# Third PSUM bank for the first mixing in the last chunk, and x of the first batch and its first MLP products ahead of that chunk

## The chip, the cores and the metric

The kernel runs on one core of a Trainium2 chip. The metric is the device time of one execution in microseconds (us), as a median over runs. Five engines work side by side, each in the order in which its instructions are written: PE (TensorE, matrix products), DVE (VectorE), ACT (ScalarE), POOL (GpSimd), and SP, which here only issues DMA transfers. They wait for each other through semaphores. PSUM, into which PE writes its products, has eight banks of 2 KiB per partition.

## The reference

Talking-heads attention over 4 batches, 12 heads, 448 positions and head size 64, and then an MLP over its 1792 tokens (768 to 2048 to 768), all in float32:

```
scores = scale * np.matmul(q, k.transpose(0, 1, 3, 2))
scores = np.einsum('bhij,hg->bgij', scores, w_pre)
scores = scores - np.max(scores, axis=-1, keepdims=True)
attn = np.exp(scores)
attn = attn / (np.sum(attn, axis=-1, keepdims=True) + 1e-09)
attn = np.einsum('bhij,hg->bgij', attn, w_post)
x = np.matmul(attn, v)        # then heads are joined: (B * S, H * D)
...
h = x @ w_in
r = np.maximum(h, 0.0)
out = (s * (r * r) + b) @ w_out
```

## The kernel before

**Tiling.** A batch's 448 rows are cut into four chunks of 110, 110, 110 and 118 rows, 16 chunks (0 to 15) in all; a chunk is cut into blocks of up to 10 rows x 12 heads, which fill 120 partitions. There are 180 blocks, 0 to 179; the last chunk, 15, has blocks 168 to 179 (the last two have 108 partitions). Step `s` of one long loop (L775 to L808) begins the first mixing of block `s` and carries the earlier blocks on.

**A block's way.** `relayout` (five steps ahead) has SP load a block of scores (`blk`); `split` (two steps ahead) has POOL cut it into a high and a low half (`hl`, L555 and L556). `premix(s)` is the first mixing: three PE products into a PSUM bank `pm` (L568), DVE's maximum over a row (L570), ACT's exponential with its sum (L575) and a small ACT operation on the sum (L579). In the next step `normalize(s-1)` takes the reciprocal on DVE (L587) and has ACT write the high half of the result, `eh` (L589); `remainder(s-1)` has DVE write its low half (L596), which is the last reading of the bank. `postmix(s-2)`, the second mixing, is 12 small products with `eh` (L611), and `evacuate(s-3)` copies them to `A`, on DVE (L627), for the last chunk on ACT (L625). AV products, `xp` (L509), turn a chunk's `A` and `v` into x^T, which ACT scales to `xs` (L523) and SP writes to memory (`xd`, L528).

**Banks.** The first mixing takes turns among three banks (two `pm`, one `px`) in all chunks but the last, where it has the two `pm` alone (L565).

**The MLP's beginning.** Three of the MLP's first products, called the head (`ph_head`, for the first batch and f = 0, 1, 2; each has six pieces, kc = 0 to 5, of three PE products), are put into the attention's last steps. The two scores banks are free by then and hold f = 0 and 1; `px` holds f = 2, whose pieces come after the last block. They need x of the first batch: `load_x` reads it back (`xraw`, L210), `split_x` has ACT write its high half (L224) and puts the low half (a DVE subtraction, L233) on a list that `low_parts` empties in the next step, between `normalize` and `evacuate`. x of the second batch takes the same `xraw` buffers, so its load waits for that subtraction. After step 168 DVE also converts MLP weights, three operations in a step (L155 to L178), until 10 units are done.

**What sets the order.** Each engine's order is that of the code. AV pairs and head pieces are spread over the steps by a planner (`fill`): a piece has a wanted step, a first and a last step and a cost, and a step takes pieces until 1.33 are spent. `tail` is 168.

Of the kernel before, what the change touches and what calls it, by code (L numbers as in the profile page):

```python
# [21 lines left out]
def talking_heads_attention__then__act_relu2_kernel(  # L22
# [27 lines left out]
    NKC = DM // P  # L50
# [11 lines left out]
    NCH = len(chunks)  # L62
# [3 lines left out]
    first = []  # L66
# [9 lines left out]
    NB = len(blocks)  # L76
# [106 lines left out]
    def convert_step(upto):  # L183

        if done["run"] is None:
            if done["conv"] >= min(upto, len(units)):
                return False
            done["run"] = conversion(done["conv"])
        try:
            next(done["run"])  # L190
        except StopIteration:
            done["run"] = None
            done["conv"] += 1
        return True
# [13 lines left out]
    def load_x(r, b, kc):  # L208
        raw = rp.tile([P, S], F32, tag="xraw", name=f"xraw_{r}_{b}_{kc}", bufs=NKC)
        nc.sync.dma_start(raw, xd[b][kc])  # L210
        xraw_t[r, b, kc] = raw

    def split_x(r, b, kc):
        raw = xraw_t.pop((r, b, kc))
        if b == 1:

            if kc % 2 == 0:
                x_u["g"] = mp.tile(
                    [P, 2, PT], F32R, tag=f"g{kc // 2}_1", name=f"xg_{r}_{kc}", bufs=1
                )  # L220
            x = x_u["g"][:, :, kc % 2 * S:kc % 2 * S + S]
        else:
            x = rp.tile([P, 2, S], F32R, tag="x", name=f"x_{r}_{b}_{kc}", bufs=NKC)
        nc.scalar.activation(x[:, 0, :], raw, AF.Copy)  # L224
        later.append((x[:, 1, :], raw, x[:, 0, :]))
        x_u[r, b, kc] = x
# [3 lines left out]
    def low_parts():  # L230
        while later:
            o, x, hi = later.pop(0)
            nc.vector.tensor_tensor(out=o, in0=x, in1=hi.bitcast(F32), op=ALU.subtract)  # L233
# [35 lines left out]


    NHEAD = 3
    head_t, head_todo = {}, [(f, kc) for f in range(NHEAD) for kc in range(NKC)]

    def head_piece():
        if not head_todo:
# [267 lines left out]
    def relayout(t):  # L543
        ci, i0, ni = blocks[t]
        blk = blkp.tile([BP, S], F32, tag="blk", name=f"blk_{t}", bufs=LD)
        nb = first[ci + 1] - first[ci]
        r = t - first[ci]
        nc.sync.dma_start(blk[:ni * H, :], s_t[ci][r:r + nb * (ni - 1) + 1:nb, :, :])
        blk_t[t] = blk

    def split(t):
        n = blocks[t][2] * H
        blk = blk_t.pop(t)
        hl = blkp.tile([BP, 2, S], F32R, tag="hl", name=f"hl_{t}", bufs=2)
        nc.gpsimd.tensor_scalar(hl[:n, 0, :], blk[:n], 1.0, 0.0, op0=ALU.mult, op1=ALU.add)  # L555
        nc.gpsimd.tensor_tensor(  # L556
            out=hl[:n, 1, :], in0=blk[:n], in1=hl[:n, 0, :].bitcast(F32), op=ALU.subtract
        )
        hl_t[t] = hl

    def premix(t):
        n = blocks[t][2] * H
        hl = hl_t.pop(t)

        tag = "px" if t % 3 == 2 and t < first[NCH - 1] else "pm"  # L565
        pm = ps.tile([P, 512], F32, tag=tag, name=f"pm_{t}", bufs=banks.count(tag))
        for m, (w, x) in enumerate(((wpre_lo, 0), (wpre_hi, 1), (wpre_hi, 0))):
            nc.tensor.matmul(pm[:n, :S], w[:n, :n], hl[:n, x, :], start=(m == 0), stop=(m == 2))  # L568
        st = smp.tile([BP, 4], F32, tag="st", name=f"st_{t}")
        nc.vector.tensor_reduce(  # L570
            out=st[:n, 0:1], in_=pm[:n, :S], axis=AX.X, op=ALU.max, negate=True
        )

        e = pm[:, :S]
        nc.scalar.activation(e[:n], e[:n], AF.Exp, bias=st[:n, 0:1], accum_out=pm[:n, S:S + 1])  # L575
        e_t[t] = (e, st)

        total = pm[:, S:S + 1]
        nc.scalar.activation(  # L579
            st[:n, 2:3], total[:n], AF.Identity, scale=2.0 ** -15, bias=tiny[:n]  # L580
        )

    def normalize(t):

        n = blocks[t][2] * H
        e, st = e_t[t]
        nc.vector.reciprocal(st[:n, 3:4], st[:n, 2:3])  # L587
        eh = blkp.tile([BP, 2, S], F16, tag="eh", name=f"eh_{t}", bufs=2)
        nc.scalar.activation(eh[:n, 0, :], e[:n], AF.Copy, scale=st[:n, 3:4])  # L589
        eh_t[t] = eh  # L590

    def remainder(t):
        n = blocks[t][2] * H
        e, st = e_t.pop(t)
        eh = eh_t[t]
        nc.vector.scalar_tensor_tensor(  # L596
            out=eh[:n, 1, :], in0=e[:n], scalar=st[:n, 3:4], in1=eh[:n, 0, :],
            op0=ALU.mult, op1=ALU.subtract,
        )

    def postmix(t):
        ci, i0, ni = blocks[t]
        n = ni * H
        eh = eh_t.pop(t)
        if i0 == 0:
            a_t[ci] = ap_.tile([P, NC, H, CH], F32, tag="A", name=f"A_{ci}")
        po = ps.tile([P, 512], F32, tag="po", name=f"po_{t}", bufs=2)
        for c in range(NC):
            j0 = min(c * P, S - P)
            for m, (x, y) in enumerate(((1, 0), (0, 1), (0, 0))):  # L610
                nc.tensor.matmul(  # L611
                    po[:, c * BP:(c + 1) * BP],
                    eh[:n, x, j0:j0 + P],
                    wpost[:n, y].rearrange("p g i -> p (g i)"),
                    start=(m == 0),
                    stop=(m == 2),
                )
        po_t[t] = po

    def evacuate(t):  # L620
        ci, i0, ni = blocks[t]
        dst = a_t[ci][:, :, :, i0:i0 + ni]
        src = po_t.pop(t)[:, :NC * BP].rearrange("p (c g i) -> p c g i", c=NC, g=H)[:, :, :, :ni]
        if ci == NCH - 1:
            nc.scalar.activation(dst, src, AF.Copy)  # L625
        else:
            nc.vector.tensor_copy(dst, src)  # L627

    LD, LS = 5, 2
# [9 lines left out]
    def at(step, order, f, *args):  # L639
        plan.append((step, order, len(plan), f, args))  # L640
# [16 lines left out]
    fill = []  # L657
    for ci in range(2, NCH):
        b, _, _ = chunks[ci]
        w0 = first[ci - 1] - LD  # L660
# [4 lines left out]
        for p in range(NP):  # L665
            when = w0 + p * (w1 - w0) / NP
# [6 lines left out]
    for ci in range(NCH):  # L673
        b = chunks[ci][0]
        w0 = first[ci + 1] + 3
        w1 = first[ci + 2] + 3 if ci + 2 <= NCH else NB + 100
        if ci == NCH - 1:
            w0 = NB + 3
        for p in range(NP):
            when = w0 + p * min(w1 - w0, 12) / NP  # L680
            fill.append((when, w0, w1 - 1, AV_COST, 1, av_pair, (ci, p)))
            if b + 1 < B and chunks[ci + 1][0] != b:
                at(w0 + (p + 1) * (w1 - w0) / NP, 2, load_v, b + 1, p)
    w0 = first[NCH - 1] + 3
    for i in range(NHEAD * NKC):
        if i < NHEAD * NKC - LATE:
            when = w0 + i * (NB + 3 - w0) / (NHEAD * NKC - LATE)
            fill.append((when, w0, NB + 2, 0.567, 1, head_piece, ()))
        else:
            fill.append((NB + 100, NB + 3, NB + 100, 0.567, 1, head_piece, ()))  # L690
    fill.sort(key=lambda x: x[0])
    spent, closed = 0.0, {}
    for s in range(NB + 4):
        spent = max(spent, -0.4) + load.get(s, 0)
        left, held = [], set()
        for x in fill:
            _, lo, hi, cost, order, f, args = x
# [16 lines left out]
        fill = left  # L714
# [5 lines left out]
    def run_plan(step, early):  # L720

        k0 = state["next"]
        while k0 < len(plan) and plan[k0][0] < step + 1:
            _, order, _, f, args = plan[k0]
            if (order == 0) == early:
                f(*args)
            k0 += 1
        if not early:
            state["next"] = k0
# [44 lines left out]
    tail = first[NCH - 1]  # L774
    for s in range(NB + 3):  # L775
        if s == tail - LD:
            early.close()
            rp = ctx.enter_context(tc.tile_pool(name="rp", bufs=1, side="right", reuse_waits="tile"))
            for n in range(NU_EARLY, NU_EARLY + NU_TAIL):
                w_pool[n] = rp  # L780
        if s + LD < NB:
            relayout(s + LD)
        if s + LS < NB:
            split(s + LS)
        if 0 <= s - 1 < NB:
            if s >= CONV0:
                convert_step(NU_EARLY)

            if s > tail:
                for _ in range(2):  # L790
                    convert_step(NU_EARLY + 3)
            normalize(s - 1)
        low_parts()
        if 0 <= s - 3 < NB:
            evacuate(s - 3)
        if s < NB:
            premix(s)
        if 0 <= s - 1 < NB:
            remainder(s - 1)
        run_plan(s, True)  # L800
        if 0 <= s - 2 < NB:
            postmix(s - 2)
        run_plan(s, False)
        if 0 <= s - (tail - LD) < NKC:
            load_x(0, 0, s - (tail - LD))
        if 0 <= s - tail < NKC:
            split_x(0, 0, s - tail)
            load_x(0, 1, s - tail)  # L808
    run_plan(NB + 100, True)
    run_plan(NB + 100, False)  # L810
    att.close()
# [101 lines left out]
```

## Time and profile before

| | |
|---|---|
| median of 3 runs | 987.62 us (987.14 to 990.37) |
| profiled execution, first to last instruction | 987.8 us |
| busy: PE, DVE, ACT, POOL | 95%, 65%, 62%, 40% |
| attention with the head, about | 0 to 520 us |

The profiled execution's own time is its span; it lies 0.2 us over the median. Busy shares are averages over the attention, where all engines work, and the MLP, in which PE hardly pauses. A time at the start of a row is in us from the first instruction. The granted clock is the share of TensorE's full clock (2.4 GHz) that it was given; 0.50 is its lower level, 1.2 GHz.

### The profile page before, as it was taken

What the parts mean: (1) busy time and instruction counts of PE and PEld (TensorE: products, weight loads), DVE (VectorE), ACT (ScalarE), POOL (GpSimd) and SP (SyncE); (2) the same over time, 40 slices, a digit from 0 to 9 for tenths busy, and PEclk for the clock granted to TensorE, in tenths of its full rate; (3) what the DMA queues carried; (4) which work ended last, traced back from release to release, by engine and by line L of the source; (5) the groups of instructions that cost most, each with busy time, mean ns of one, the idle gap of its engine ahead of it and who ended that gap; (6) DMA issues with size and microseconds to landing.
All of it is one profiled execution on the core that took longest, in us unless ns stands there. A gap on an engine that the chain in (4) does not pass through costs nothing.

```text
span 987.8 us, 19819 instructions
## 1 busy us (share of the span) xinstructions
PE 935.6 (95%) x7500; PEld 792.3 (80%) x7500; DVE 641.9 (65%) x1314; ACT 607.9 (62%) x1315; POOL 399.3 (40%) x469
## 2 busy tenths in 40 slices
PE   6798999989999999999799999999999999999998
PEld 3566777757777677777578999899998999999998
DVE  4689999977877787888945605937624911748411
ACT  3587878877888788887658778622215687721000
POOL 2666667756676666767423333200001232310000
PEclk9899999999999999999799999999999999999999
DMA  3565544664346543544511412325441330236521
GB/s 87 150 177 140 142 126 132 173 153 128 103 123 159 131 134 102 141 128 136 168 56 38 142 34 77 92 91 158 134 155 33 106 119 1 64 113 187 164 94 53
DMA packets 124222, 114.63 MB, mean 116 GB/s; under 512 B 61626, under 2 KB 120014, under 8 KB 124126
## 3 DMA queue, kind: packets, MB, share of 16 engines
q1 hardware_dynamic: 115902, 102.26, 37.3%
q10 hardware_dynamic: 8064, 11.01, 3.1%
q8 instruction: 59, 0.97, 0.4%
q0 software_dynamic: 160, 0.09, 0.2%
q14 instruction: 37, 0.30, 0.1%
HBM read 58.28 MB, written 16.52 MB: 76 GB/s over the span
## 4 chain that ended last, share of the span: by engine, by line
PE 52%; ACT 21%; DVE 18%; DMA 5%; issue 2%; SPq 1%; POOL 1%; ACTq 0%; DVEq 0%; POOLq 0%
PE po L300 23%; PE ph L248 16%; ACT pm L575 6%; ACT S L495 5%; DVE st L570 4%; PE xp L509 4%; PE pm L568 3%; DVE A L627 3%; ACT eh L589 3%; ACT st L579 2%; DMA blk<-S 2%; PE sc L485 2%; PE po L611 2%; DVE eh L596 2%; DVE raw L172 1%
## 5 line engine op out<-in xcount | busy, mean ns | idle before, releaser
L300 PE MATMUL po<-w,g 128*128 128x384 f32 x1344 | 234.6, 336 | 2.6 <-ACT h L256 2.6
L300 PEld LDWEIGHTS po<-w,g 128*128 128x128 f32 x1344 | 233.6, 188 | 3.3 <-ACT h L256 3.2
L556 POOL TENSOR_TENSOR hl<-blk,hl 120x448 fp32r<-120x448 f32 x180 | 207.5, 1153 | 15.0
L266 POOL TENSOR_TENSOR g<-h,g 128x448 fp32r<-128x448 f32 x64 | 77.2, 1206 | 293.9 <-ACT g L265 275.4
L555 POOL TENSOR_SCALAR hl<-blk 120x448 fp32r<-120x448 f32 x180 | 105.0, 583 | 158.3 <-PE pm L568 137.4
L248 PE MATMUL ph<-x,w 128*128 128x448 f32 x810 | 166.2, 364 | 0.0
L611 PEld LDWEIGHTS <-eh 120*128 120x128 f16 (+1 forms) x2160 | 118.0, 99 | 56.0 <-DVE eh L596 27.0
L248 PEld LDWEIGHTS ph<-x,w 128*128 128x128 f32 x810 | 152.0, 188 | 12.2
L611 PE MATMUL po<-wpost,eh 120*128 120x120 f16 (+1 forms) x2160 | 148.2, 220 | 10.5 <-DVE eh L596 10.2
L575 ACT ACTIVATE pm<-pm,st 120x448 f32<-120x448 f32 x180 | 109.7, 609 | 76.3 <-DVE st L570 75.4
L596 DVE SCALAR_TENSOR_TENSOR eh<-pm,st,eh 120x448 f16<-120x448 f32 x180 | 122.1, 678 | 15.0 <-ACT eh L589 10.9
L589 ACT ACTIVATE eh<-pm,st 120x448 f16<-120x448 f32 x180 | 114.5, 636 | 15.2 <-DVE st L587 14.2
L570 DVE TENSOR_REDUCE st<-pm 120x1 f32<-120x448 f32 x180 | 110.8, 616 | 11.5 <-PE pm L568 10.9
L627 DVE COPY A<-po 128x480 f32<-128x480 f32 x168 | 107.3, 639 | 0.1
L568 PE MATMUL pm<-hl,wpre_hi 120*120 120x448 f32 x360 | 104.4, 372 | 1.8 <-POOL hl L556 1.8
L485 PE MATMUL sc<-Tk,Tq 64*110 64x448 f32 (+1 forms) x576 | 84.9, 401 | 13.1 <-ACT S L495 6.1
L509 PE MATMUL xp<-A,v 128*64 128x110 f32 (+1 forms) x1536 | 92.3, 266 | 1.0 <-ACT xs L523 1.0
L154 ACT ACTIVATE mk<-raw 128x384 f32<-128x384 f32 x64 | 35.4, 553 | 92.8 <-DMA raw<-in_moe_w_out_dram 38.1
L568 PE MATMUL pm<-hl,wpre_lo 120*120 120x448 f32 x180 | 84.3, 468 | 5.9 <-DVE eh L596 5.3
L495 ACT ACTIVATE S<-sc 110x896 f32<-110x896 f32 (+1 forms) x90 | 82.1, 912 | 8.8 <-PE sc L485 5.4
L509 PEld LDWEIGHTS xp<-A,v 128*64 128x64 f32 x1536 | 74.8, 137 | 15.7 <-issue 8.5
L568 PEld LDWEIGHTS pm<-hl,wpre_hi 120*120 120x120 f32 x360 | 67.0, 187 | 7.2 <-POOL hl L556 2.8
(72 smaller groups left out, 971.3 us busy)
## 6 DMA issues: line engine op xcount, KB each, us to landing
blk<-S SPq DMA_DIRECT2D x172, 210.0 KB
raw<-in_moe_w_in_dram SPq DMA_DIRECT2D x32, 384.0 KB
raw<-in_moe_w_out_dram SPq DMA_DIRECT2D x32, 384.0 KB
xraw<-xd SPq DMA_DIRECT2D x48, 224.0 KB
part<-ob ACTq DMA_DIRECT2D x28, 192.0 KB
acc<-part SPq DMA_DIRECT2D x28, 192.0 KB
out_dram<-acc ACTq DMA_DIRECT2D x28, 192.0 KB
v<-in_v_dram SPq DMA_DIRECT2D x24, 192.0 KB
```

Source lines behind the costliest of these rows:

```text
L248: nc.tensor.matmul(ph[:, :S], w[:, i, c0:c0 + P], x[:, y, :], start=(kc == 0 and m == 0), stop=(kc == NKC - 1 and m == 2),)
L300: nc.tensor.matmul(po[:, :NO], g[:, x, c0:c0 + P], w[:, y, :], start=(f == 0 and m == 0), stop=(f == NF - 1 and m == 2),)
L495: nc.scalar.activation(s_t[ci][:n, 2 * p:2 * p + 2, :], x_t["two"][:n, :, :S], AF.Copy, scale=SCALE)
L509: nc.tensor.matmul(xp[e * D:(e + 1) * D, p % 4, :n], vt[:, e, c, :], a[:, c, 2 * p + e, :n], start=(c == 0), stop=(c == NC - 1),)
L556: nc.gpsimd.tensor_tensor(out=hl[:n, 1, :], in0=blk[:n], in1=hl[:n, 0, :].bitcast(F32), op=ALU.subtract)
L568: nc.tensor.matmul(pm[:n, :S], w[:n, :n], hl[:n, x, :], start=(m == 0), stop=(m == 2))
L570: nc.vector.tensor_reduce(out=st[:n, 0:1], in_=pm[:n, :S], axis=AX.X, op=ALU.max, negate=True)
L575: nc.scalar.activation(e[:n], e[:n], AF.Exp, bias=st[:n, 0:1], accum_out=pm[:n, S:S + 1])
L589: nc.scalar.activation(eh[:n, 0, :], e[:n], AF.Copy, scale=st[:n, 3:4])
L596: nc.vector.scalar_tensor_tensor(out=eh[:n, 1, :], in0=e[:n], scalar=st[:n, 3:4], in1=eh[:n, 0, :], op0=ALU.mult, op1=ALU.subtract,)
L611: nc.tensor.matmul(po[:, c * BP:(c + 1) * BP], eh[:n, x, j0:j0 + P], wpost[:n, y].rearrange("p g i -> p (g i)"), start=(m == 0), stop=(m = ...
L627: nc.vector.tensor_copy(dst, src)
```

## The change

Four edits. The first mixing takes the third bank (`px`) in the last chunk too. The loads of x of the first batch are issued two in a step, in steps 163 to 165 (before: one in a step, 163 to 168). Its split begins in step 166 (before: 168), and the loads of the second batch's x with it. The planner gives head pieces of f = 0 and 1 in turns by kc (before: all of f = 0, then f = 1), from step 167 on (before: 171).

```
-    head_t, head_todo = {}, [(f, kc) for f in range(NHEAD) for kc in range(NKC)]
+    head_t = {}
+    head_todo = [(f, kc) for kc in range(NKC) for f in range(2)] + [(2, kc) for kc in range(NKC)]
...
-        tag = "px" if t % 3 == 2 and t < first[NCH - 1] else "pm"
+        tag = "px" if t % 3 == 2 else "pm"
...
-    w0 = first[NCH - 1] + 3
+    w0 = first[NCH - 1] - 1
     for i in range(NHEAD * NKC):
         if i < NHEAD * NKC - LATE:
             when = w0 + i * (NB + 3 - w0) / (NHEAD * NKC - LATE)
-            fill.append((when, w0, NB + 2, 0.567, 1, head_piece, ()))
+            fill.append((when, w0 + i // 2, NB + 2, 0.567, 1, head_piece, ()))
...
-        if 0 <= s - (tail - LD) < NKC:
-            load_x(0, 0, s - (tail - LD))
-        if 0 <= s - tail < NKC:
-            split_x(0, 0, s - tail)
-            load_x(0, 1, s - tail)
+        if 0 <= 2 * (s - (tail - LD)) < NKC:
+            load_x(0, 0, 2 * (s - (tail - LD)))
+            load_x(0, 0, 2 * (s - (tail - LD)) + 1)
+        if 0 <= s - (tail - 2) < NKC:
+            split_x(0, 0, s - (tail - 2))
+            load_x(0, 1, s - (tail - 2))
```

On PE, around the beginning of the last chunk, before (names end in a block, then a running number; `x_0_0_0` is piece kc = 0 of x; "..." stands for the other products of the second mixings):

```order
L611 MATMUL po_165_7674<-wpost_127,eh_165_7619 128x120
L568 MATMUL pm_168_7698<-hl_168_7615,wpre_lo_126 120x448
L568 MATMUL pm_168_7698<-hl_168_7615,wpre_hi_125 120x448 x2
...
L611 MATMUL po_166_7707<-wpost_127,eh_166_7662 128x120
L568 MATMUL pm_169_7742<-hl_169_7658,wpre_lo_126 120x448
```

And of the change, the same place:

```order
L612 MATMUL po_165_7683<-wpost_127,eh_165_7625 128x120
L248 MATMUL ph_head_7696<-x_0_0_0_7660,w_0_828 128x448 x3
L248 MATMUL ph_head_7696<-x_0_0_0_7660,w_2_1456 128x448 x3
L569 MATMUL pm_168_7717<-hl_168_7621,wpre_lo_126 120x448
L569 MATMUL pm_168_7717<-hl_168_7621,wpre_hi_125 120x448 x2
...
L612 MATMUL po_166_7726<-wpost_127,eh_166_7670 128x120
L248 MATMUL ph_head_7696<-x_0_0_1_7703,w_0_828 128x448 x3
L248 MATMUL ph_head_7696<-x_0_0_1_7703,w_2_1456 128x448 x3
L569 MATMUL pm_169_7765<-hl_169_7666,wpre_lo_126 120x448
```

Two head pieces now stand ahead of mixings 168 and 169; one each stands ahead of 170 and 171, which had none. Behind the mixing 179 there were three pieces (kc = 3, 4, 5 of f = 1) and an AV pair; now there are none until the last chunk's AV products.

On DVE, in steps 167 and 168, before:

```order
L587 RECIPROCAL st_166_7626<-st_166_7626 120x1
L627 COPY A_14_7357<-po_164_7631 128x48x10
L570 TENSOR_REDUCE st_167_7669<-pm_167_7665 120x1
L596 SCALAR_TENSOR_TENSOR eh_166_7662<-pm_166_7622,st_166_7626,eh_166_7662 120x448
L587 RECIPROCAL st_167_7669<-st_167_7669 120x1
L627 COPY A_14_7357<-po_165_7674 128x48x10
L570 TENSOR_REDUCE st_168_7702<-pm_168_7698 120x1
```

And of the change:

```order
L588 RECIPROCAL st_166_7632<-st_166_7632 120x1
L233 TENSOR_TENSOR x_0_0_0_7660<-xraw_0_0_0_7536,x_0_0_0_7660 128x448
L628 COPY A_14_7357<-po_164_7637 128x48x10
L571 TENSOR_REDUCE st_167_7678<-pm_167_7674 120x1
L597 SCALAR_TENSOR_TENSOR eh_166_7670<-pm_166_7628,st_166_7632,eh_166_7670 120x448
L588 RECIPROCAL st_167_7678<-st_167_7678 120x1
L233 TENSOR_TENSOR x_0_0_1_7703<-xraw_0_0_1_7538,x_0_0_1_7703 128x448
L628 COPY A_14_7357<-po_165_7683 128x48x10
L571 TENSOR_REDUCE st_168_7721<-pm_168_7717 120x1
```

The low halves of x come in between the reciprocal and the copy of `A`, two steps earlier than before; in steps 173 and 174, where the last two stood, there are none.

On ACT, in the last two steps, before (`xs_14_7850` is the second part of chunk 14's x^T):

```order
L589 ACTIVATE eh_178_8165<-pm_178_8130,st_178_8134 108x448
L625 ACTIVATE A_15_7790<-po_176_8139 128x48x10
L575 ACTIVATE pm_179_8168<-pm_179_8168,st_179_8172 108x448
L579 ACTIVATE st_179_8172<-pm_179_8168,tiny_129 108x1
L523 ACTIVATE xs_14_7850<-xp_14_4_8152,xscale_128 128x2x110
L589 ACTIVATE eh_179_8204<-pm_179_8168,st_179_8172 108x448
```

And of the change:

```order
L524 ACTIVATE xs_14_7879<-xp_14_4_8100,xscale_128 128x2x110
L590 ACTIVATE eh_178_8184<-pm_178_8148,st_178_8152 108x448
L626 ACTIVATE A_15_7816<-po_176_8157 128x48x10
L576 ACTIVATE pm_179_8187<-pm_179_8187,st_179_8191 108x448
L580 ACTIVATE st_179_8191<-pm_179_8187,tiny_129 108x1
L590 ACTIVATE eh_179_8210<-pm_179_8187,st_179_8191 108x448
```

The scaling of chunk 14's x^T has moved from ahead of the last `eh` to ahead of the one before it.

## Rows read from the trace of the kernel before

**Rows 1.** The page's first part: busy time, share of the span, instructions.

```profile
PE 935.6 (95%) x7500; PEld 792.3 (80%) x7500; DVE 641.9 (65%) x1314; ACT 607.9 (62%) x1315; POOL 399.3 (40%) x469
```

**Rows 2.** Windows: length, busy us of PE, PEld, DVE, ACT, POOL, clock, DMA share, GB/s.

```profile
470.00:475.00 5.00, 1.28 (x14) 1.05 (x13) 4.96 (x11) 3.25 (x9) 1.97 (x3) 0.61 0.74 216
...
480.00:485.00 5.00, 5.00 (x34) 4.04 (x33) 3.57 (x8) 3.17 (x8) 1.65 (x2) 0.52 0.58 173
```

**Rows 3.** Chain of waits, 440 to 520 us: total us, times, longest us.

```profile
POOL hl L555 <- PE pm L568: 21.0, 17, 4.4
...
PE pm L568 <- DVE eh L596: 5.3, 5, 2.9
```

**Rows 4.** Timeline of PE: start us, us (overlapping), instruction, count, idle before it.

```profile
474.90 0.70 PE L568 MATMUL pm<-hl,wpre_lo 120*120 120x448 f32 x1 [2.88 <-DVE eh L596]
...
500.40 1.46 PE L248 MATMUL ph_head<-x,w 128*128 128x448 f32 x6
501.70 0.36 PE L568 MATMUL pm<-hl,wpre_lo 108*108 108x448 f32 x1
...
502.32 0.81 PE L611 MATMUL po<-wpost,eh 120*128 120x120 f16 x12
503.05 0.97 PE L509 MATMUL xp<-A,v 128*64 128x110 f32 x16
...
510.89 3.45 PE L509 MATMUL xp<-A,v 128*64 128x118 f32 x64
```

**Rows 5.** Timeline of DVE, 467 to 506 us.

```profile
467.30 0.61 DVE L570 TENSOR_REDUCE st<-pm 120x1 f32<-120x448 f32 x1
...
469.58 0.61 DVE L570 TENSOR_REDUCE st<-pm 120x1 f32<-120x448 f32 x1
...
471.09 1.38 DVE L159 SCALAR_TENSOR_TENSOR u<-raw,u 128x384 uint32<-128x384 uint32 x1
...
473.55 0.61 DVE L570 TENSOR_REDUCE st<-pm 120x1 f32<-120x448 f32 x1
...
474.67 0.34 DVE L163 TENSOR_SCALAR raw<-raw 128x384 uint32<-128x384 uint32 x1
...
475.41 0.55 DVE L172 SCALAR_TENSOR_TENSOR raw<-raw 128x384 uint32<-128x384 uint32 x1
...
475.95 0.60 DVE L233 TENSOR_TENSOR x<-xraw,x 128x448 fp32r<-128x448 f32 x1
476.48 0.64 DVE L627 COPY A<-po 128x480 f32<-128x480 f32 x1
477.04 0.61 DVE L570 TENSOR_REDUCE st<-pm 120x1 f32<-120x448 f32 x1
...
485.13 0.62 DVE L570 TENSOR_REDUCE st<-pm 120x1 f32<-120x448 f32 x1 [1.53 <-PE pm L568]
...
505.48 0.62 DVE L570 TENSOR_REDUCE st<-pm 108x1 f32<-108x448 f32 x1 [1.11 <-PE pm L568]
```

**Rows 6.** Timeline of SP: the issue of one load of x.

```profile
459.35 0.50 SPq L210 DMA_DIRECT2D xraw<-xd  x1
```

**Rows 7.** Timeline of ACT, 466 to 508 us.

```profile
466.53 0.44 ACT L523 ACTIVATE xs<-xp,xscale 128x220 f32<-128x220 f32 x1
...
471.10 0.57 ACT L224 ACTIVATE x<-xraw 128x448 fp32r<-128x448 f32 x1
...
507.71 0.45 ACT L523 ACTIVATE xs<-xp,xscale 128x220 f32<-128x220 f32 x1 [0.61 <-PE xp L509]
```

**Rows 8.** Timeline of POOL: two subtractions.

```profile
467.24 1.14 POOL L556 TENSOR_TENSOR hl<-blk,hl 120x448 fp32r<-120x448 f32 x1
...
470.76 1.29 POOL L556 TENSOR_TENSOR hl<-blk,hl 120x448 fp32r<-120x448 f32 x1
```

**Rows 9.** Groups by line, 440 to 520 us: count, busy us, mean ns, idle before.

```profile
L159 DVE SCALAR_TENSOR_TENSOR u<-raw,u 128x384 uint32<-128x384 uint32 x3 | 2.9, 982 | 0.1
L172 DVE SCALAR_TENSOR_TENSOR raw<-raw 128x384 uint32<-128x384 uint32 x3 | 2.6, 869 | 0.0
```

## The prediction

> **What bounds the kernel now.** I read the page first: PE is busy for 95% of the span [rows 1], so only places where PE stands still or runs slowly can give time back. The windows show one such place. From 470 to 475 us PE is busy for 1.28 of 5.00 us at a mean granted clock of 0.61, and from 480 to 485 us it is busy throughout at 0.52 [rows 2]. 0.50 is the lower of the clock's two levels (1.2 of 2.4 GHz), so the clock fell at 475 - 5 x 0.39 / 0.5 = 471.1 us and rose at 480 + 5 x 0.48 / 0.5 = 484.8 us: 13.7 us at half rate. This is the beginning of the last chunk. The chain of waits names the cause: PE's first mixing waits 5.3 us in five places for DVE's `eh` L596 (the remainder, which frees the bank), 2.9 us of it at once [rows 3]. In order of time: at 474.90 PE starts a mixing after 2.88 us of standing still, and its products take 0.70 us each [rows 4]; at 485.13 DVE, which had not paused since 469.58 but for its own work, waits 1.53 us for PE [rows 5].
>
> I number DVE's reductions (L570) by their step: 167 starts at 467.30, 168 at 469.58, 169 at 473.55, 170 at 477.04, 172 at 485.13, 179, the last, at 505.48 [rows 5]. PE starts the last chunk's AV products (`xp_15`) at 510.89 [rows 4]. From there to the end the order of instructions is the same in both programs, so what is won by then should be won at the end.
>
> **The change part by part.** *The loads of x.* They come in pairs, the last one three steps earlier; one costs 0.50 us on SP [rows 6], so the next `blk` loads start 0.5, 1.0 and 1.5 us later. The loads of the second batch now stand ahead of `blk` loads while they wait for the x remainders. I cost both at nothing: POOL, which consumes `blk`, waited 21.0 us in this stretch for PE [rows 3], up to 4.4 us at once, and that is the cover. Without it a late `blk` would cost its lateness, about 1.5 us once.
>
> *The split of x, two steps earlier.* Six ACT copies and six DVE remainders, as before. Later they lay beside conversion work; in steps 167 and 168 there is none. On DVE the remainder now stands between the reciprocal and the copy of `A`, and it waits for ACT's copy. In step 167 ACT first has `xs` (466.53, 0.44), then the copy of x (0.57) [rows 7], ending near 467.45. With the remainder (0.53, from 475.95 to 476.48) and the `A` copy (0.56, to 477.04) [rows 5] the reduction starts near 468.55 in place of 467.30: +1.25. In step 168 it is +0.9: 0.53, and some 0.4 of waiting (the copy's 0.57 less about 0.15 after which the reciprocal could start). So +2.2 at reduction 168.
>
> That is the lower bound, because DVE also meets POOL. L159 at 471.09 took 1.38 us [rows 5] while a POOL subtraction ran from 470.76 for 1.29 [rows 8], and it ended 0.42 after it: the DVE operation did nothing until POOL was done. In step 167 POOL has such a subtraction from 467.24 to 468.38 [rows 8]; a remainder held until then ends near 468.85, which makes step 167 +2.1 and the sum +3.0. I take +2.6. The Trainium skill (SBUF — State Buffer, section "SBUF: two separate sides") calls the port pair of VectorE and GpSimd an exclusive lock, held for a whole instruction, also against a VectorE operation with two SBUF inputs, as x's remainder is. By that rule this term is the full +3.0 and the sum below 0.4 worse; the trace's row agrees.
>
> *The head's products, ahead of the chunk.* Two pieces stand before mixing 168 and two before 169, one before 170 and 171: 0.65 us each (a pair from 500.40 to 501.70 [rows 4]). PE was ahead of DVE there, so they cost nothing until they must wait for x's remainder; PE then stands still until the remainder is done (468.0 to 468.9) before the first pair and 0.5 to 2 us in each of the steps after, where it stood 2.88 at once. They leave the steps from 177 on: three pieces fewer behind mixing 179.
>
> *The third bank.* Mixing 170 no longer waits for the remainder of 168. This wait is removed, but by itself it moves DVE little, since DVE is the late engine there; what it gives is that PE does not stop for 2.88 us, and, if that was what cost the clock, full rate afterwards.
>
> **The sum** follows DVE from reduction 168, new at 469.58 + 2.6 = 472.2. A step of DVE that never waits: from 473.55 to 477.04 it is 3.49, of which the reduction and the remainder take 1.12 (to 474.67), three conversion operations and the reciprocal 1.28 (to 475.95), x 0.53, `A` 0.56 [rows 5]. Step 168 to 169 took 3.97 with the collision; the collision was about 0.8, so 3.15. After it come 3.49, and without `A` (ACT has it then) 2.93 and 2.93: 12.5 to reduction 172. Collisions can be anything from none to 0.8 in each of these eight steps. In the old order L159 and L172, three of each, averaged 0.98 and 0.87 us here [rows 9], where an undisturbed L172 took 0.55 (at 475.41 [rows 5]): an excess of 3 x (0.43 + 0.32) = 2.2. I take 0.2 a step, 1.6 in all, somewhat less, since two of x's remainders are out of this stretch. Reduction 172 is then at 472.2 + 12.5 + 0.8 = 485.5, where it was 485.13: the late start is just made up, as DVE doesn't wait for a slow PE. From 172 on x's remainders are gone from DVE: 2.40 a step (3.49 less 0.56 and 0.53), or 2.05 with two conversion operations in place of three, so 8.9 to reduction 176, with 0.8 for collisions 495.2.
>
> Then conversions end and PE binds. Mixing is 0.62 at 108 rows, I estimate 0.70 at 120 from it; the second mixing 0.73, AV 0.97, a head piece 0.65 [rows 4]. Step 177: 0.70 + 0.73 + 0.97 + 0.65 = 3.05; 178: 0.62 + 0.73 + 0.65 = 2.00; 179: 0.62 + 0.73 + 0.97 + 0.65 = 2.97. Reduction 179 is at 495.2 + 8.0 = 503.2, 2.3 before 505.48. Last, `xs` of chunk 14 no longer stands ahead of the last `eh` on ACT: at 507.71 it had waited 0.61 for PE, then took 0.45 [rows 7]; ACT was idle from 507.10, the reciprocal needs some 0.2 of that, so about 0.7. Total -2.3 - 0.7 = -3.0 us. The profiled span is 987.8, and the median of the timed runs is 987.62, 0.2 under it: 984.8 by the one, **984.6** by the other. As a check, PE has from mixing 168 to 179 12 mixings (8.2), 11 second mixings (8.0), 6 AV (5.8) and 10 pieces (6.5), 28.5 us, in the 33 us from about 470.2 to 503.2: 4.5 us of slack.
>
> **Rivals.** (1) *The clock falls all the same.* PE still stops briefly in every step from 167 to 171, up to 2 us as worked out above, and 2.88 us went with the fall before. Against it: PE has twice the work in steps 167 and 168. With 13.7 us at half rate PE does 6.85 us less, the slack takes 4.5, and 2.35 of the gain is lost: -0.65, 987.0. The Trainium skill (TensorE: Matmul & The Clock Gate, section "A second HAM failure mode: psum-queue depth-cycling") tells of a kernel whose short stops between groups, while it cycled through PSUM banks, made the clock go back and forth; by that rule this is the outcome. The rows show one fall and one rise here, no going back and forth. (2) *DVE stays the bound and the wait goes over to x.* POOL now splits right behind mixings that PE gives earlier, in the midst of DVE's conversions. With reduction 168 at +3.0 and twice the collisions (0.4 a step, 3.2 in place of 1.6) the gain is 3.0 - 0.4 - 1.6 = 1.0: 986.6. For it speaks that DVE had almost no pause from 469.58 to 485. (3) *Slower: the clock stays low for longer.* It is the place of (1), and each further microsecond at half rate costs 0.5: from 15 us on (7.5 - 4.5 = 3.0) nothing is left of the gain, at 20 us it is +2.5, 990.1. Against it: PE has more queued work than before, which let the clock rise at 484.8.
>
> **How the numbers follow.** Forecast 52% (its own range 983.0 to 985.8: the two bounds of the late start, collisions from none to 3.2, PE ahead or not at 176), rival 1 28%, rival 2 13%, rival 3 7%. What a measurement here can tell from no change is 0.3%, 3.0 us, so the line is 984.66, in the middle of the forecast. Of the forecast I put 35 of 52 points under it, since PE may be up to 0.7 ahead at 176 and collisions may be fewer than I took; with 5 points from rival 1, for a fall that is much shorter, that is faster 40%, slower 5% (most of rival 3), the same 55%. The range from 983.2 to 987.4 leaves out the best of the forecast and rival 3.
>
> **What would show it.** Right: a granted clock of 1.00 from 465 to 505; no wait of PE's L569 for `eh` over 1 us; reduction 168 two to three us later than 469.58, 172 level, 179 and `xp_15` two to four earlier; the same distance from `xp_15` to the end. Wrong: a stretch at 0.50 between 470 and 495 (rivals 1 and 3), DVE operations of L155 to L178 and L233 well over their usual time in most steps (rival 2), POOL waiting for `blk`, or a distance from `xp_15` to the end that has changed.

## The result, and the profile after

The change makes the kernel slower: 993.34 us in the median (991.29 to 997.51, 6 runs) against 987.62 (987.14 to 991.07), a ratio of 1.0052 with a 95% interval of 1.0036 to 1.0069, some 5 us. The forecast was 3 us the other way. The profiled execution spans 995.8 us, at the slow end of its runs; 2.7 us of that lie ahead of everything that the change touches (a fall of the clock between 204 and 211 us; the profiled execution of the kernel before has none there, and six of the sixteen in the experiments have one), so all that follows counts from reduction 166, the last that is the same in both.

| from, to | before, us | forecast, us | after, us |
|---|---|---|---|
| reduction 166 to 168 | 4.57 | 7.2 | 7.61 |
| 168 to 172 | 15.55 | 13.3 | 15.73 |
| 172 to 176 | 12.48 | 9.7 | 13.04 |
| 176 to 179 | 7.87 | 8.0 | 8.68 |
| 179 to the last chunk's AV products (`xp_15`) | 5.41 | 4.7 | 4.75 |
| from there to the end | 476.91 | 476.9 | 478.27 |
| sum of the differences from before | | -3.0 | +5.3 |

The starts are those of L570 in the kernel before and of L571 in the changed one, whose lines stand one further on. The lag at 168 came about as forecast, but the chunk never made it up, and the end became longer.

Why the chunk did not make it up shows in DVE's timeline of the changed kernel, between reductions 169 and 170:

```profile
478.78 0.61 DVE L571 TENSOR_REDUCE st<-pm 120x1 f32<-120x448 f32 x1
479.31 0.67 DVE L597 SCALAR_TENSOR_TENSOR eh<-pm,st,eh 120x448 f16<-120x448 f32 x1
479.90 0.35 DVE L163 TENSOR_SCALAR raw<-raw 128x384 uint32<-128x384 uint32 x1
480.17 0.90 DVE L168 SCALAR_TENSOR_TENSOR w<-mk,u 128x384 fp32r<-128x384 f32 x1
480.99 1.51 DVE L172 SCALAR_TENSOR_TENSOR raw<-raw 128x384 uint32<-128x384 uint32 x1
482.43 0.15 DVE L588 RECIPROCAL st<-st 120x1 f32<-120x1 f32 x1
482.50 0.90 DVE L233 TENSOR_TENSOR x<-xraw,x 128x448 fp32r<-128x448 f32 x1
483.32 0.65 DVE L628 COPY A<-po 128x480 f32<-128x480 f32 x1
483.89 0.61 DVE L571 TENSOR_REDUCE st<-pm 120x1 f32<-120x448 f32 x1
```

And in POOL's, at the same time:

```profile
479.92 0.75 POOL L556 TENSOR_SCALAR hl<-blk 120x448 fp32r<-120x448 f32 x1 [0.62 <-PE pm L569]
480.75 1.34 POOL L557 TENSOR_TENSOR hl<-blk,hl 120x448 fp32r<-120x448 f32 x1
482.21 0.72 POOL L556 TENSOR_SCALAR hl<-blk 120x448 fp32r<-120x448 f32 x1
483.01 1.38 POOL L557 TENSOR_TENSOR hl<-blk,hl 120x448 fp32r<-120x448 f32 x1
```

The step takes 5.11 us in place of 3.49 [rows 5]. L168 ends 0.40 after POOL's first operation, L172 0.41 after the second, x's remainder 0.47 after the third. Undisturbed, L172 takes 0.55 and x's remainder 0.60 [rows 5], so each did most of its work only when POOL was through. The kernel before did the same three conversions from 474.67 on [rows 5] while POOL stood still, waiting for a mixing:

```profile
476.44 0.57 POOL L555 TENSOR_SCALAR hl<-blk 120x448 fp32r<-120x448 f32 x1 [4.38 <-PE pm L568]
```

In the changed kernel the third bank lets PE give mixings 170 and 171 within 2.3 us, and POOL cuts two blocks in a row, right among DVE's conversions. By groups, over the chunk (line, count, busy us, mean ns):

```profile
L233 DVE TENSOR_TENSOR x<-xraw,x 128x448 fp32r<-128x448 f32 x6 | 5.0, 839 | 0.9 <-ACT x L224 0.9
L172 DVE SCALAR_TENSOR_TENSOR raw<-raw 128x384 uint32<-128x384 uint32 x3 | 4.1, 1381 | 0.0
...
L168 DVE SCALAR_TENSOR_TENSOR w<-mk,u 128x384 fp32r<-128x384 f32 x3 | 2.4, 789 | 0.0
```

L172 takes 1.38 us in the mean, where it was 0.87 [rows 9] and 0.55 when nothing is in its way. PE's mixings no longer wait for `eh`, where it was 5.3 us [rows 3]. But between 440 and 520 us its second mixings wait 8.8 us for it in eight places, where it was 3.0 in five. By PE's timeline:

```profile
471.61 1.48 PE L248 MATMUL ph_head<-x,w 128*128 128x448 f32 x6 [1.76 <-DVE x L233]
...
485.15 1.38 PE L612 MATMUL po<-wpost,eh 120*128 120x120 f16 x12 [3.02 <-DVE eh L597]
...
516.11 0.80 PE L612 MATMUL po<-wpost,eh 108*128 108x120 f16 x12 [1.24 <-DVE eh L597]
517.53 5.11 PE L510 MATMUL xp<-A,v 128*64 128x118 f32 x64 [0.62 <-ACT A L626]
```

The stop of 2.88 us ahead of mixing 170 [rows 4] is gone, and 3.02 us ahead of second mixing 169 has come. And `xp_15` takes 5.11 us in place of 3.45 [rows 4], since the clock falls in it; the windows (as in rows 2):

```profile
485.00:490.00 5.00, 4.85 (x45) 4.40 (x46) 4.88 (x13) 4.21 (x12) 0.00 (x0) 0.50 0.49 151
...
515.00:520.00 5.00, 3.27 (x43) 3.11 (x45) 0.68 (x1) 1.79 (x4) 0.00 (x0) 0.81 0.02 3
520.00:525.00 5.00, 4.09 (x65) 3.87 (x64) 0.00 (x0) 0.81 (x2) 0.00 (x0) 0.84 0.11 30
```

From 470 us on the clock is low for some 13.6 us in all, about as long as before (13.7), but in three pieces: 6.8 us from 484.0, 3.4 from 504.5, and 3.4 from 518.1, behind the chunk.

### The profile page after: what moved, and what is told of

Its sections match the earlier page's. It is cut to its first block, busy times and chain, and to the rows that moved or that the text cites. A ratio compares the mean times of both kernels' runs of the same rounds, so it can differ in the third digit from the quotient of the medians.

```text
span 995.8 us, 19811 instructions
## 1 busy us (share of the span) xinstructions
PE 939.5 (94%) x7500; PEld 796.8 (80%) x7500; DVE 644.6 (65%) x1314; ACT 607.9 (61%) x1315; POOL 400.4 (40%) x469
## 5 line engine op out<-in xcount | busy, mean ns | idle before, releaser
L557 POOL TENSOR_TENSOR hl<-blk,hl 120x448 fp32r<-120x448 f32 x180 | 207.9, 1155 | 15.0
L571 DVE TENSOR_REDUCE st<-pm 120x1 f32<-120x448 f32 x180 | 110.7, 615 | 13.1 <-PE pm L569 12.4
L486 PE MATMUL sc<-Tk,Tq 64*110 64x448 f32 (+1 forms) x576 | 85.5, 403 | 13.3 <-ACT S L496 6.7
L510 PE MATMUL xp<-A,v 128*64 128x110 f32 (+1 forms) x1536 | 95.4, 272 | 1.5 <-ACT xs L524 0.9
L510 PEld LDWEIGHTS xp<-A,v 128*64 128x64 f32 x1536 | 77.9, 142 | 16.1 <-issue 8.9
L233 DVE TENSOR_TENSOR x<-xraw,x 128x448 fp32r<-128x448 f32 x36 | 22.8, 660 | 77.5 <-ACT x L224 77.5
```

The lines of the kernel that those rows point to most:

```text
L510: nc.tensor.matmul(xp[e * D:(e + 1) * D, p % 4, :n], vt[:, e, c, :], a[:, c, 2 * p + e, :n], start=(c == 0), stop=(c == NC - 1),)
L557: nc.gpsimd.tensor_tensor(out=hl[:n, 1, :], in0=blk[:n], in1=hl[:n, 0, :].bitcast(F32), op=ALU.subtract)
L571: nc.vector.tensor_reduce(out=st[:n, 0:1], in_=pm[:n, :S], axis=AX.X, op=ALU.max, negate=True)
```

## The experiments

A ratio is to the kernel before, run on the same chip in the same turns (its median there was 989.0 to 989.5 us). "168" and "179" are the distances from reduction 166, "tail" is that from `xp_15` to the end, all three from one profiled execution of each kernel; before has 4.57, 40.47 and 476.91, the change 7.61, 45.06 and 478.27. "Held time" is what DVE's conversions and x's remainders took between reductions 168 and 176 above 0.35 us (conversions with one input), 0.55 (with two) and 0.60 (x), which they take undisturbed; before has 3.2 us, the change 5.0. The expectations name their theories by letters: L for the lag at reduction 168, C for the collisions of POOL with DVE, K for the clock.

**One part at a time.** The bank alone, in the kernel before:

```
-        tag = "px" if t % 3 == 2 and t < first[NCH - 1] else "pm"
+        tag = "px" if t % 3 == 2 else "pm"
```

> The kernel before with the third bank alone; x and the head's pieces as before. Theory L (the loss comes from x's split in steps 167 and 168, where DVE has no other work beside it: it put reduction 168 3.0 us later in the changed kernel): no lag here and the wait of 2.88 us gone, so 1 to 3 us faster than before, 985 to 986.6. Theory C (the loss comes from POOL's splits, which follow mixings that PE gives earlier and hold DVE's conversions; these took 2.8 us more in the changed kernel): the bank alone lets PE ahead, so 0 to 3 us slower, 987.6 to 990.6. Theory K (the clock falls more often because PE's stops are spread): nothing but a clock that falls tells, several stretches at 0.50 from 470 on, and the time follows their length.

Measured 0.9998 (0.9990 to 1.0007): 168 4.57, 179 39.46, tail 476.82. No gain and no loss. L's gain of 1 to 3 us for the bank did not come; C's "no better" held, though at its edge. The trace shows a trade: from reduction 166 to 179 DVE waits 0.4 us for PE in place of 3.2, but the held time is 4.6 us in place of 3.2, and DVE waits 1.1 us for ACT's `eh` in place of 0.2.

The loads and the split of x alone, in the kernel before (the change's last hunk):

> The kernel before with x's loads in pairs and x's split two steps earlier alone; two banks, the head's pieces as before. Theory L: reduction 168 3 us later than before against reduction 166, and at least half of it still there at the end: 1.5 to 4 us slower, 989 to 991.6. Theory C: the bank is what matters, so as before within 1 us, since the two remainders of x that leave steps 173 and 174 pay for those that come to 167 and 168. Theory K: as before, PE's stops are the same.

Measured 1.0030 (1.0019 to 1.0042): 168 7.44, 179 40.86. This version is slower, as L had it, but that the early split is the reason is not shown. In its profiled execution only 0.4 us of the lag are left at 179. This execution spans 989.3 us, 1.5 more than that of the kernel before, and 1.4 of these lie ahead of reduction 166 (466.44 against 465.01), where its clock fell between 200 and 210 us (0.88 and 0.78 in two windows of 5 us) and that of the kernel before did not.

The change without its bank:

> The changed kernel with the bank edit undone: two banks in the last chunk, x and the pieces early. Theory L: still slow, 991 to 994. Theory C: mixings wait for remainders again and POOL's splits fall beside DVE's reductions and remainders of eh rather than its conversions, so 1 to 4 us faster than the changed kernel, 989 to 992. Theory K: mixing waits for eh again, a stop more, so slower than the changed kernel by up to 2 us.

Measured 1.0008 (0.9997 to 1.0019): 168 7.54, 179 39.93, tail 478.71. So on top of the other edits the bank costs some 4.4 us by the ratios, though alone it costs nothing. DVE's groups in this run:

```profile
L168 DVE SCALAR_TENSOR_TENSOR w<-mk,u 128x384 fp32r<-128x384 f32 x3 | 1.7, 551 | 0.0
L172 DVE SCALAR_TENSOR_TENSOR raw<-raw 128x384 uint32<-128x384 uint32 x3 | 1.6, 550 | 0.0
...
L233 DVE TENSOR_TENSOR x<-xraw,x 128x448 fp32r<-128x448 f32 x6 | 5.4, 897 | 0.9 <-ACT x L224 0.9
```

With two banks L168 and L172 are not held at all; x's remainders are, but the held time is 1.8 us in place of 5.0, and DVE's waits for PE up to reduction 179 are 2.0 in place of 3.6. These two make 4.8 of the 5.1 us by which 179 comes earlier. This speaks for C, against L (still slow, 991 to 994; it was 989.97) and against K (a stop more, and yet faster). The same holds in all twelve traces in which POOL's work, the conversions and the engine of x's remainders are as in the two kernels: their held time is 1.7 to 3.2 us in the seven with two banks and 4.3 to 5.7 in the five with three.

The change with x and the pieces at their old times (the third bank and the order by kc stay):

> The changed kernel with x's loads and split and the pieces' first step as in the kernel before (171); the third bank and the order of the pieces by kc stay. Theory L: no lag, so 1 to 3 us faster than before, 985 to 986.6, like the bank alone. Theory C: like the bank alone too, but 0 to 3 us slower than before. If it differs from the bank alone by over 1 us, the order of the pieces counts, for which no theory stands yet.

Measured 1.0008 (0.9999 to 1.0017): 168 4.56, 179 40.06, tail 477.03. Like the bank alone within 1 us, again without L's gain; the order by kc shows no effect.

**Conversions out of the chunk**, from the changed kernel and from the one before:

```
-            if s > tail:
-                for _ in range(2):
-                    convert_step(NU_EARLY + 3)
```

> The changed kernel without weight conversions in steps 169 to 179 (units 7 to 9 are converted at the MLP's beginning in their place, where DVE stands still for some 9 us). Theory C (POOL's splits hold DVE's conversions, and with the third bank they fall together): the chunk loses its 10 us of conversion work and the 4 us by which it was stretched, so it is PE that binds: reduction 179 some 36 us after reduction 166 in place of 45, and 4 to 8 us faster than the changed kernel, 985 to 989. Theory L (the lag of 3 us in steps 167 and 168 is what stays): reduction 168 still 7.6 after 166, and only the conversions' own time less. Theory K (the clock): still two or more falls after 470.

> The kernel before with the same removal of the conversions from the last chunk. If DVE's conversions are what bounds the chunk, this gains 2 to 4 us over before (985 to 987 where before is 989). By theory C it should come out within 1 us of the changed kernel without conversions, since what parted the two were collisions; by theory L it should be 2 to 3 us faster than that.

Measured 1.0049 (1.0034 to 1.0065) and 1.0032 (1.0017 to 1.0047). In the chunk C's numbers came: 179 at 36.78 and 37.25, so the conversions cost the changed kernel 8.3 us there and the kernel before 3.2, and without them the two are alike. But the time was given back: tail 485.79 and 482.94. The MLP's beginning could not take them for nothing, as these expectations had it, so neither gain came; and by the ratios the two lie 1.7 us apart, not within 1. Windows of the first:

```profile
525.00:530.00 5.00, 1.53 (x4) 1.42 (x5) 4.65 (x11) 2.47 (x5) 0.14 (x1) 0.50 0.33 98
```

PE works 1.53 of 5.00 us there, at half clock, while DVE converts.

**POOL's subtraction out of the chunk**, from the changed kernel:

```
+        if blocks[t][0] == NCH - 1:
+            nc.gpsimd.memset(hl[:n, 1, :].bitcast(F32), 0.0)
+        else:
             nc.gpsimd.tensor_tensor(
...
```

> The changed kernel with POOL's subtraction L557 left out for the last chunk's blocks (the low half of their scores is set to zero, a write without a read; PE's products stay). Theory C: DVE's conversions go undisturbed (L172 0.55 to 0.75 us in the mean in place of 1.38), reduction 179 some 40 to 42 us after 166 in place of 45, and 2.5 to 4 us faster than the changed kernel. If what stretches the chunk is something else (the bank's turn, the clock), as the changed kernel within 1 us.

Measured 1.0001 (0.9988 to 1.0014), 5 us better than the changed kernel by the ratios: 179 37.67, tail 479.03, held time 0.7 us. DVE's group again:

```profile
L172 DVE SCALAR_TENSOR_TENSOR raw<-raw 128x384 uint32<-128x384 uint32 x3 | 1.6, 550 | 0.0
```

PE's and DVE's work is that of the change. Only what POOL does became another (and shorter: 0.47 us in place of 1.14), and the chunk is 7.4 us shorter, which is more than C had said. That POOL's shorter work let PE go earlier is not the reason: in the chunk of the changed kernel PE waits nowhere for POOL. This is the most direct test of C.

**The pieces behind the last mixings**, put back in the changed kernel:

```
+            lo = w0 + i // 2
+            if i >= 9:
+                when = lo = NB + i - 10
```

> The changed kernel with the last three of the twelve early pieces put back behind the second mixings 177, 178 and 179, as in the kernel before. Theory T (the pieces were what kept PE at work while it waits for the last remainders; without them the clock falls again during the last chunk's AV products): the fall at 518 to 522 us is gone, the distance from the first AV product of the last chunk to the end is 476.9 in place of 478.3, and the kernel is 1 to 2 us faster than the changed one. If the pieces don't matter there, as the prediction had it: the same time within 0.5 us.

Measured 1.0022 (1.0011 to 1.0032), 3 us better: tail 476.73. Its window:

```profile
515.00:520.00 5.00, 4.09 (x57) 3.62 (x52) 0.14 (x1) 2.17 (x6) 0.00 (x0) 1.00 0.18 48
```

The clock stays at 1.00 through `xp_15`. The chunk became shorter too (179 at 42.52), with fewer pieces ahead of the last mixings.

**x's remainders on POOL**, in the change and in the kernel before (`nc.gpsimd.tensor_tensor` in `split_x`):

> The changed kernel with x's remainders of the first batch on POOL in place of DVE. Theory L: the lag of 3 us at reduction 168 is gone (reduction 168 at 4.6 to 5 us after reduction 166 in place of 7.6) and with it 2 to 3 us of the time. Theory C: POOL works more, so collisions with the conversions stay or grow; within 1.5 us of the changed kernel.

> The kernel before with x's remainders of the first batch on POOL in place of DVE, at their old time. If DVE's work is what bounds the chunk: 3.2 us less of it, so 1.5 to 3 us faster than before. Theory C: POOL's new subtractions hold the conversions as its splits do, so within 1 us of before, with L159 to L178 well over 0.55 us.

Measured 1.0018 (1.0004 to 1.0033) and 1.0005 (0.9994 to 1.0016). In the change 168 falls to 5.81 and 3.4 us are won by the ratios: L's side, since C had said at most 1.5. In the kernel before nothing is won, as C had it, and L168 goes to 1.51 us in the mean: what DVE is spared POOL takes back by holding it (held time 7.1 and 5.9 us).

**The mends together.** Two banks and cover (the last three pieces behind the last mixings again), in the changed kernel; then x's remainders on POOL as well:

> The changed kernel with both mends: two banks in the last chunk (no collisions) and the last three pieces back behind mixings 177 to 179 (cover). If the two causes are separate, the gains add: 4.4 + 2.5 us off the changed kernel's 5.2 over before, so 0.5 to 2.5 us faster than before; reduction 179 40 us after 166, 476.8 from the last chunk's first AV product to the end. If the lag of 3 us by x's early split counts for itself, it is no better than before.

> As the run with two banks and cover, and x's remainders of the first batch on POOL. Theory L: another 1 to 3 us faster than without, since reduction 168 comes 1.5 to 3 us earlier. Theory C: POOL's six subtractions of 1.15 us fall beside conversions again, so no faster, or up to 1.5 us slower.

Measured 0.9986 (0.9976 to 0.9997), faster than before, and 1.0012 (1.0001 to 1.0023). The two mends add, to 1.4 us over before where the sum had been 2.2: 179 at 39.03, tail 476.43. POOL as the place for x makes it worse again, in C's direction, by 2.6 us where C had allowed 1.5.

**The lag.** x's remainders in the last chunk behind the remainder of `eh`, with both mends and without:

```
-        low_parts()
+        if s <= tail - 2:
+            low_parts()
...
             remainder(s - 1)
+        if s > tail - 2:
+            low_parts()
```

> As the run with two banks and cover, and in the last chunk x's remainders stand behind DVE's remainder of eh in place of ahead of the copy of A, so no reduction stands behind them in their own step. Theory L (x's remainders ahead of the copy of A make reductions 167 and 168 late, and this lag stays): reduction 168 at 4.6 to 5.2 us after 166 in place of 7.5, 1 to 3 us faster than the run with two banks and cover, 2 to 4.5 us faster than before. Rival: the lag is made up by other waits, since PE has to wait for x in any case: within 0.7 us of that run.

> The changed kernel with x's remainders in the last chunk behind the remainder of eh, third bank and pieces as in the change. Theory L: reduction 168 at 4.6 to 5.2 us after 166 in place of 7.6 and 2 to 3 us faster than the changed kernel (2 to 3 us over before is left, by the collisions and the tail). Rival: conversions collide all the more as PE gets further ahead, so within 1 us of the changed kernel.

Measured 1.0030 (1.0017 to 1.0042) and 1.0051 (1.0035 to 1.0066). Theory L, as stated, falls: reduction 167 is back at 2.28, but 168 is at 7.13 and 8.12 all the same. In the first of the two DVE now waits for PE (2.31 us), because in PE's queue the first head pieces stand ahead of mixing 168 and wait for x:

```profile
469.44 1.73 PE L248 MATMUL ph_head<-x,w 128*128 128x448 f32 x6 [2.12 <-DVE x L233]
470.97 0.58 PE L569 MATMUL pm<-hl,wpre_lo 120*120 120x448 f32 x1
...
472.33 0.62 DVE L571 TENSOR_REDUCE st<-pm 120x1 f32<-120x448 f32 x1 [2.31 <-PE pm L569]
```

So two more, which also give the pieces one step later (`lo = w0 + 1 + i // 2`), with x's remainders behind and ahead:

> Two banks, cover, x's remainders behind the remainder of eh, and the early head pieces one step later (the first pair ahead of mixing 169). Theory P (the lag comes from PE: a head piece that waits for x stands ahead of the mixing in PE's queue, 2.12 us in the run without this): reduction 168 at 4.6 us after 166, and 1 to 4 us faster than the run with two banks and cover. Theory L (DVE's order): the same expectation, since neither is left. If the lag is not lost in either, reduction 179 stays at 39 us or more and the time within 0.7 us of that run.

> Two banks, cover, and the pieces one step later; x's remainders ahead of the copy of A as in the change. Theory P: reduction 168 at 5 to 6 us after 166 and 1 to 3 us faster than the run with two banks and cover. Theory L: reduction 168 at 7.5 as there, since DVE's order is the same, and the time within 0.7 us.

| two banks and cover | pieces as in the change | pieces a step later |
|---|---|---|
| x ahead of the copy of `A` | 0.9986; 168 at 7.54 | 0.9986 (0.9976 to 0.9996); 168 at 7.56 |
| x behind the remainder of `eh` | 1.0030; 168 at 7.13 | **0.9976 (0.9963 to 0.9988); 168 at 4.74** |

Either place alone makes the lag: on DVE, x ahead of the copy of `A`; on PE, pieces ahead of a mixing before x is there. It goes only when both are mended, so both L and P were half right. What the lag costs is less than L had it: between the two versions with x ahead and the last one, 1.1 us at 179 (39.03 and 39.06 against 37.93), and 0.9976 is not clear of 0.9986. The last version, at 986.51 us (before 988.97 beside it), beats both kernels by its interval. Its profiled execution, whose clock shows no fall in the chunk:

```profile
470.00:475.00 5.00, 3.81 (x28) 3.07 (x27) 4.96 (x11) 3.70 (x11) 3.01 (x3) 1.00 0.57 185
...
480.00:485.00 5.00, 4.03 (x63) 3.31 (x63) 4.49 (x11) 3.08 (x8) 3.27 (x4) 1.00 0.51 157
```

## Why the prediction was wrong, step by step

*What bounds the kernel: half right.* The stretch from 470 to 485 us was the right place, and DVE was the engine that is late there. But the 2.88 us stop was not what cost the clock. The kernel before is already slow in the second mixing at 470.85, ahead of that stop, behind two shorter ones:

```profile
468.56 0.81 PE L611 MATMUL po<-wpost,eh 120*128 120x120 f16 x12 [0.76 <-DVE eh L596]
...
470.85 1.17 PE L611 MATMUL po<-wpost,eh 120*128 120x120 f16 x12 [0.83 <-DVE eh L596]
```

*The loads of x at nothing: right by the trace.* All of POOL's waits between 440 and 520 us, 25.7 us in 17 places, still end on PE.

*The late start: right in its place, its upper bound was the value.* Reduction 168 came 3.04 us later; 2.6 was taken, 3.0 is what the held remainder gave:

```profile
470.16 1.40 DVE L233 TENSOR_TENSOR x<-xraw,x 128x448 fp32r<-128x448 f32 x1 [0.64 <-ACT x L224]
```

Its second cause, pieces that wait on PE, was named in words ("stands still until the remainder is done") and given no price of its own; the table above shows that it alone would have made nearly the same lag (7.13).

*The third bank, and with it the sum from 168 to 176: this is the step that failed.* The prediction had it that "by itself it moves DVE little, since DVE is the late engine there; what it gives is that PE does not stop for 2.88 us". Alone it did move DVE little (0.9998), and in the changed kernel the clock did stay up longer, to 484.0 in place of 471.1. But PE's stop was taken for a mere loss. It also kept POOL still while DVE converted, and much of what was seen as POOL's cover of 21.0 us of waiting was the room in which DVE worked undisturbed. So the bank had no price on DVE in the sum, and on top of the early x and pieces it cost 4.4 us.

*The sum's collisions, where that price belonged: mis-sized.* 0.2 us a step, 1.6 in all, was taken from the old order. The held time was 5.0: L172 lost 3 x 0.83 = 2.5 against 0.55, L159 and L168 0.8 and 0.7, x's last four remainders 0.5 against 0.60, the others 0.4. (x's first two lost 0.9 more, ahead of reduction 168; that is part of the late start.) From 168 to 176 the forecast was missed by 2.4 + 3.3 = 5.8 us, of the 8.3 that lie between -3.0 and +5.3. The collisions are 3.4 of these 5.8, and 1.07 is DVE's wait for the slow PE at reduction 172; the sum had no wait of DVE there. The remaining 1.3 are not taken apart. Rival 2 had this mechanism at twice the allowance, with a gain of 1.0 left. It was three times the allowance, and it did not come alone: the late start was missed by 0.4, the steps from 176 to 179, where the clock falls again, by 0.7, and the tail by 1.4. The 0.7 us for `xs` came true (5.41 to 4.75).

*"The same distance from `xp_15` to the end": wrong.* The three pieces behind mixing 179 were called fewer instructions. They were the work that kept PE going between the last remainders. All five traces without them that keep the conversions in the chunk have tails of 478.3 to 479.0 us, and the eleven with them 476.3 to 477.0. The prediction looked for a fall of the clock in steps 167 to 171 alone, though it named a changed distance among the signs of being wrong.

*Rival 1 and its rule.* The clock did go back and forth (three pieces in place of one), which is the form that the rule of the Trainium skill (TensorE: Matmul & The Clock Gate, section "A second HAM failure mode: psum-queue depth-cycling") gives to short stops between groups. The trace agrees in part: the third fall, at 518.1, came behind short stops (1.24 and 0.62 us the last), but the first came in a stop of 3.02 us and the second behind one of 1.90. And the low time from 470 us on was the same, 10.2 us of it in the chunk in place of 13.7, so it does not explain the loss in the chunk. *Rival 3*, a longer low clock, did not happen, though its sign did.

*Open:* why the version with the early split of x alone is 3 us slower while its profiled execution shows 0.4 of it at reduction 179; why the version with both mends and x behind the remainder of `eh` came to 1.0030, while from reduction 166 to the end its profiled execution, the fastest of its ten, takes no longer than that of the kernel before; and how much of the difference between runs of one kernel (some 4 us) is where the clock falls.

## What to carry to other kernels

An engine's wait can be what keeps it out of another's way: before a wait is removed, see what the engine behind it (here POOL behind PE's mixing) will do earlier, and with what it shares. A piece that fills a hole must not stand ahead of the critical instruction before its own input is surely there: here one step later was 5.3 us better with x behind (0.9976 against 1.0030; 3.3 us of it, from reduction 166 to the end, show in the two profiled executions), and nothing with x ahead. And work that leaves the end of a stretch takes its cover with it.

## What the runs showed of the hardware

Behind a POOL operation that reads SBUF and had begun first, DVE's operations with two SBUF inputs (L159, L168, L172, L178 and x's remainders) had to wait: in both kernels each that took longer than undisturbed ended 0.40 to 0.48 us after such an operation. Two conversions with one input that took longer (L163 at 492.94 in the kernel before, 0.82 us in place of 0.34, and L176 at 503.04 in the changed one, 0.48 in place of 0.35) ended 0.20 and 0.21 after one. POOL is held in turn: in the rows above L557 takes 1.34 and 1.38 us, where it takes 1.14 undisturbed [rows 8]. DVE's operations that read PSUM are not held: reduction, remainder of `eh` and copy of `A` kept 0.61, 0.68 and 0.64 us in the mean in both kernels.

POOL's write without a read did not hold DVE either. In the run without POOL's subtraction L168 ended 0.41 us after the operation that reads, while the write was still running:

```profile
476.35 0.91 DVE L168 SCALAR_TENSOR_TENSOR w<-mk,u 128x384 fp32r<-128x384 f32 x1
...
476.16 0.69 POOL L556 TENSOR_SCALAR hl<-blk 120x448 fp32r<-120x448 f32 x1 [1.75 <-issue]
476.80 0.47 POOL L558 MEMSET hl<- 120x448 f32 x1
```

The rule of the Trainium skill that the prediction named (SBUF — State Buffer, section "SBUF: two separate sides") has it that a VectorE operation with two SBUF inputs meets the lock only against a GpSimd operation that reads SBUF, and that whichever starts first has it for the whole instruction. These rows agree. The prediction used the rule for the late start alone; the rest of the sum had 0.2 us a step.
